# Attention scores that leave PSUM with their minimum: what does it do to the time?

## The chip, the cores and the metric

The kernel runs on one core of a Trainium2 chip. A time is the device time of one execution in microseconds. Before the change, three runs had a median of 697.19 us (697.01 to 699.52).

## The reference

q, k and v have shape (4, 8, 576, 64): batch, heads, sequence, head size. The reference rotates q and k by position, forms attention for each head, joins the heads to x of (4, 576, 512), and sends x through a token mixer and a channel mixer:

```
scores = (q_rot @ k_rot.T) / 8
scores = scores - max(scores, axis=-1)
attn   = exp(scores);  attn = attn / (sum(attn, axis=-1) + 1e-9)
x = attn @ v                                  # heads joined: (4, 576, 512)
u = x + (relu(x.T @ w_tok1) @ w_tok2).T       # 576 -> 256 -> 576
out = u + relu(u @ w_ch1) @ w_ch2             # 512 -> 1536 -> 512
```

The mixers' weights come as float64 and are split on the chip into pairs of fp32r values.

## The kernel before, in words

Attention goes over 16 pairs of heads. `prep` loads k, q and v of a pair, rotates k and q on POOL (pair 0 on DVE, L298 to L304), transposes them on PE (L327) and splits them into a high and a low part (ACT L341, DVE L344). `pair` takes the 576 rows of queries as four blocks of 128 and a tail of 64. The tail's rows of both heads are one block of 128, with block-diagonal operands made on POOL (L357). The order of blocks is 0, 1, tail, 2, 3.

For a block and each of its two heads: PE forms 128 x 576 scores in two PSUM banks (L429; the tail at L396) as three fp32r products. DVE takes the negated maximum of the row (L379), ACT the exponential with that as bias and the row's sum as an accumulator (L382), from PSUM into `p` in SBUF. PE transposes `p` in pieces of 64 (L449, tail L407), and ACT or DVE copies the pieces to `pt` (L454, L413, L420). After two or three blocks PE multiplies `pt` by v (L467, narrow with 256 columns after block 1, wide with 320 after block 3), and ACT or DVE copies the product out (L470). At the pair's end PE transposes it back (L496) and DVE scales it by 1/sum into `X` (L501, L505).

PSUM has 8 banks of 512 fp32 values for each partition. In attention two double banks (`s`) hold scores, and four single banks (`t`) hold transposes, two at a time, and P·V.

`plan` is a scheduler that runs when the program is built. Each task has an engine (or a choice of two), an estimated duration, the tasks it follows, the buffers it holds, and a priority. Repeatedly it takes, for each engine, the tasks that could start within SLACK of the earliest, and of these the one with the lowest priority. The resulting order of each engine's instructions is fixed: on the chip every engine works its queue from the front. AT holds what is added to 9 times the pair's number to make a priority. `f64_split` makes the mixers' weights; six blocks of token weights are split during attention, the channel weights during the mixers. The mixers follow in a plan of their own, with PSUM cut into 8 single banks.

Of the kernel before, what the change touches and what calls it, by code (L numbers as in the profile page):

```python
# [48 lines left out]
class Task:  # L49
    __slots__ = ("alts", "deps", "bufs", "prio", "end", "eng", "waits", "heirs", "mode")  # L50
# [5 lines left out]
class Plan:  # L56
# [8 lines left out]
    def add(self, eng, dur, fn, deps=(), bufs=(), prio=0.0, alts=(), mode="full"):  # L65
        t = Task()
        t.mode = mode
        t.alts = [(eng, dur, fn)] + list(alts)
        t.deps = [d for d in deps if d is not None]
        t.bufs = list(bufs)  # L70
        for b in t.bufs:
            b.users += 1
        t.prio = prio
        t.end = None
        t.heirs = []
        self.tasks.append(t)
        return t

    def start(self, t, eng):
# [11 lines left out]
        if eng == "PE" and t.mode != self.mode:  # L91
            s = max(s, self.clock["PE"] + SWITCH)
        return s

    def run(self):
# [10 lines left out]
        while left:  # L106
# [45 lines left out]
AT = {"qk": -239.14, "mx": 17.16, "ex": -436.59, "tr": -5.68, "eh": -55.41, "el": 296.2, "tt": -89.5, "th": -35.74, "tl": -123.52, "pv": -20.38, "p1": 280.88, "p2": -206.16, "fin": 18.15, "f6": -333.69, "load": -9.36, "rot": 238.0, "pt": -13.39, "bd": -69.91, "qkt": -64.88, "cp": 0.87, "dup": -248.71, "vs": 6.76}  # L152
FIRST = -60.0
SWITCH = 0.15
SLACK = {"PE": 0.08, "ACT": 0.06, "DVE": 0.32, "POOL": 0.17, "SP": 0.05}
# [18 lines left out]
def pool(n):  # L174
    return n * 0.00235 + 0.07
# [3 lines left out]
def rope_attention_mixer_kernel(ctx: ExitStack, tc: tile.TileContext, q, k, v, w_tok1, w_tok2, w_ch1, w_ch2, tab, out):  # L179
# [35 lines left out]
    def attention(ctx):  # L215
# [3 lines left out]
        def slots(nm, n, shape, dt=F32, pool=pers, fifo=True):  # L219
# [3 lines left out]
        raw = {"k": slots("kraw", 1, [P, 2, R + 1, D]), "q": slots("qraw", 1, [P, 2, R + 1, D]),  # L223
               "v": slots("vraw", 2, [P, 2, R + 1, D])}
# [3 lines left out]
        bds = slots("bd", 2, [P, 2, P], F32R)  # L228
# [35 lines left out]
        def prep(n):  # L264
            b, hp = divmod(n, HP)
            pos = 9 * n
            for nm, src, pr in (("k", k, 0.0), ("q", q, 0.5), ("v", v, 1.0)):
# [14 lines left out]
                pl = pos + AT["load"] + pr  # L282
# [27 lines left out]
                for r0, r1 in ((0, 2), (2, R + 1)) if n == 0 else ((0, R + 1),):  # L310
                    for i in range(4):
                        w = (r1 - r0) * 2 * D // (1 if i < 2 else 2)
                        bufs = [[rb, wb], [rb, ub], [ub, wb], [ub, wb]][i]
                        if n == 0:
                            x = [add("DVE", dve(w), rot(nc.vector, i, r0=r0, r1=r1), x, bufs, FIRST + pr + r0)]
                        else:
                            x = [add("POOL", pool(w), rot(nc.gpsimd, i), x, bufs, pos + AT["rot"] + pr)]
                    xy = [Buf(t_ps), Buf(t_ps)]
# [4 lines left out]
                    def tr(r0=r0, r1=r1, xy=xy, ub=ub, first=first):  # L323
                        for i in range(r1 - r0):
                            for z in range(2):
                                r = (i - 1) % (R + 1) if z and first else r0 + i
                                nc.tensor.transpose(xy[z].t[:, i * TL:(i + 1) * TL],  # L327
                                                    ub.t[halves[z], r].rearrange("p h d -> p (h d)"), ident[halves[z], halves[z]])

                    pp = pos + AT["pt"] + pr if n else FIRST + r0  # L330
                    t = add("PE", 0.11 * (r1 - r0), tr, x, [*xy, ub, hi, lo], pp, mode="row")
                    for z in range(2):
# [3 lines left out]
                        for o, m, i0 in parts:  # L336
                            src = lambda z=z, xy=xy, m=m, o=o: xy[z].t[:, o * TL:(o + m) * TL].rearrange("p (r s) -> p r s", s=TL)
# [8 lines left out]
                            y = add("ACT", act(m * TL), fh, [t], [xy[z], hi], pp)  # L346
                            eh.append(y)
                            el.append(add("DVE", dve(m * TL), fl, [y], [xy[z], hi, lo], pp))
                ready[n, nm] = (eh + el, hi, lo)
                if nm == "q":  # L350
                    bb = Buf(bds)
                    bdone = []
                    pp = pos + AT["bd"] + pr
# [10 lines left out]
        def pair(n):  # L364
# [13 lines left out]
            def mx(sb, nm):  # L378
                return lambda: nc.vector.tensor_reduce(out=nm.t, in_=sb.t[:, :, 0:W2], axis=AX.XY, op=ALU.max, negate=True)  # L379

            def ex(sb, nm, p, l):
                return lambda: nc.scalar.activation(out=p().rearrange("p (a b) -> p a b", a=2), in_=sb.t[:, :, 0:W2], func=ACTF.Exp,  # L382
                                                    bias=nm.t, accum_out=l())

            for i, j in enumerate(ORDER):
                g = 9 * n + 2 * i
                c = 0 if j in (0, 1) else 1
                if j is None:
                    xy = [Buf(t_ps), Buf(t_ps)]
                    sb, nm, pb = Buf(s_ps), Buf(nms), Buf(pqs)  # L390
# [6 lines left out]
                    x = add("PE", 0.81, qk, bdone + kd, [sb, bb, kh, kl], g + AT["qkt"])  # L397
                    x = add("DVE", 0.67, mx(sb, nm), [x], [sb, nm], g + AT["mx"])
                    x = [add("ACT", 0.65, ex(sb, nm, lambda pb=pb: pb.t[:, 0:S], lambda: lb.t[:, R, 0:1]),
                             [x], [sb, nm, pb, lb], g + AT["ex"])]  # L400
                    exps += x

                    def tr(pb=pb, xy=xy):
                        for r in range(R + 1):
                            for z in range(2):
                                c0 = r * P - (TL if z and r == R else 0)
                                nc.tensor.transpose(xy[z].t[:, r * TL:(r + 1) * TL], pb.t[halves[z], c0:c0 + P], ident[halves[z], halves[z]])  # L407

                    x = order_tr[0] = add("PE", 0.55, tr, [*x, order_tr[0]], [*xy, pb, pt[c]], g + AT["tr"], mode="row")
                    y = None  # L410
                    for z in range(2):
                        def cp(e, z=z, xy=xy, c=c, m=R + 1 - z):
                            return lambda: e(out=pt[c].t[:, (R + 1) * z:(R + 1) * z + m, 2 * P:2 * P + TL],  # L413
                                             in_=xy[z].t[:, 0:m * TL].rearrange("p (r s) -> p r s", r=m))

                        y0, y = y, both(cp, (R + 1 - z) * TL, [x], [xy[z], pt[c]], g + AT["cp"])
                        ev[c].append(y)

                    def cpt(e, xy=xy, c=c):
                        return lambda: e(out=pt[c].t[halves[1], R, 2 * P:2 * P + TL], in_=xy[1].t[halves[1], R * TL:(R + 1) * TL])  # L420
                    ev[c].append(both(cpt, TL, [x, y0], [xy[1], pt[c]], g + AT["cp"]))
                    continue
                sbs, nmb, pb = [Buf(s_ps), Buf(s_ps)], [Buf(nms), Buf(nms)], Buf(ps)
# [7 lines left out]
                t = add("PE", 0.8, qk, qd + kd, [*sbs, qh, ql, kh, kl], g + AT["qk"], mode="row")  # L431
                xs = []
                for h in range(2):
                    x = add("DVE", 0.67, mx(sbs[h], nmb[h]), [t], [sbs[h], nmb[h]], g + h + AT["mx"])
                    x = add("ACT", 0.65, ex(sbs[h], nmb[h], lambda h=h, pb=pb: pb.t[:, h * S:(h + 1) * S], lambda h=h, j=j: lb.t[:, j, h:h + 1]), [x],
                            [sbs[h], nmb[h], pb, lb], g + h + AT["ex"])
# [4 lines left out]
                for h in range(2):  # L441
                    xy = [Buf(t_ps), Buf(t_ps)]
                    m = R + h

                    def tr(pb=pb, xy=xy, h=h, m=m):
                        for i in range(m):
                            for z in range(2):
                                c0 = h * M + i * P
                                nc.tensor.transpose(xy[z].t[:, i * TL:(i + 1) * TL], pb.t[halves[z], c0:c0 + P], ident[halves[z], halves[z]])  # L449

                    x = order_tr[0] = add("PE", 0.11 * m, tr, [*xs[0:h + 1], order_tr[0]], [*xy, pb, pt[c]], g + h + AT["tr"], mode="row")
                    for z in range(2):
                        def cp(e, z=z, xy=xy, c=c, o=o, h=h, m=m):
                            return lambda: e(out=pt[c].t[:, R * h:R * h + m, o + z * TL:o + (z + 1) * TL],  # L454
                                             in_=xy[z].t[:, 0:m * TL].rearrange("p (r s) -> p r s", r=m))
                        ev[c].append(both(cp, m * TL, [x], [xy[z], pt[c]], g + h + AT["cp"]))
# [4 lines left out]
                ab = Buf(a_ps)  # L461

                def pv(c=c, w=w, ab=ab):
                    for r in range(R + 1):
                        for h in range(2):
                            m = pt[c].t[:, R if r == R else r + h * (R + 1), 0:w]
                            nc.tensor.matmul(ab.t[halves[h], 0:w], vb.t[:, h, r, :], m, start=(r == 0), stop=(r == R))  # L467

                def p1(e, w=w, ab=ab, c0=c0):
                    return lambda: e(out=oT.t[:, c0:c0 + w], in_=ab.t[:, 0:w])  # L470

                x = add("PE", 10 * (w / 1200 + 0.0025), pv, ev[c] + vdone, [ab, vb, pt[c]], g + AT["pv"], mode="col")
                pv_done.append(both(p1, w, [x], [ab, oT], g + AT["p1"]))

            pp = 9 * n + AT["fin"]
# [11 lines left out]
            x = add("ACT", 0.1, f1, exps, [lb], pp - 1)  # L487
            x = add("POOL", 0.1, f2, [x], [lb], pp - 0.9)
            inv = add("DVE", 0.13, f3, [x], [lb, rb], pp - 0.8)
            xy = [Buf(t_ps), Buf(t_ps)]  # L490
            cs = hp * 2 * D

            def f4():
                for j in range(R + 1):
                    for z in range(2):
                        nc.tensor.transpose(xy[z].t[:, j * D:(j + 1) * D], oT.t[halves[z], j * P:(j + 1) * P], ident[halves[z], halves[z]])  # L496

            x = add("PE", 0.55, f4, pv_done, [*xy, oT], pp, mode="row")
            for z in range(2):
                def f5(z=z):  # L500
                    nc.vector.tensor_tensor(out=X[b][:, :, cs + z * D:cs + (z + 1) * D], in0=xy[z].t[:, 0:R * D].rearrange("p (r d) -> p r d", r=R),  # L501
                                            in1=rb.t[:, 0:R, z].unsqueeze(2).to_broadcast([P, R, D]), op=ALU.mult)
# [357 lines left out]
```

## Time and profile before

| | us |
|---|---|
| median of 3 runs | 697.19 |
| the profiled execution | 696.52 |
| its span, first to last instruction | 694.7 |
| PE busy in it | 630.0 (91%) |
| DVE busy | 432.4 (62%) |
| ACT busy | 319.8 (46%) |
| POOL busy | 282.1 (41%) |

PE is TensorE's matmul, PEld its weight loads, DVE VectorE, ACT ScalarE, POOL GpSimd, SP the engine that issues most transfers. The busy shares are means over two unlike parts: attention ends near 325 us, and the mixers fill the rest.

### The profile page before, as it was taken

The page shows a single profiled execution, that of the slowest core. Times are in us where ns is not written, and L with a number is a line of the kernel's source. Part 1 is how long each engine was busy: PE and PEld are TensorE (multiplying, and loading weights), DVE is VectorE, ACT ScalarE, POOL GpSimd, SP SyncE. Part 2 cuts the span into 40 slices and gives each one's busy share as a digit, 9 for nine tenths or more (in the row PEclk, how much of TensorE's full clock was granted, in tenths as well). Part 3 has the DMA queues.
Part 4 walks back from the last instruction along what each step waited for, and adds up shares of the span by engine and source line. Part 5 has one row for each costly group of instructions (what it writes and reads, how often), then busy time and mean ns, then how long its engine had stood idle before and what let it go on. Part 6 is the DMA issues. An engine that isn't in the chain of part 4 may idle for free.

```text
span 694.7 us, 13160 instructions
## 1 busy us (share of the span) xinstructions
PE 630.0 (91%) x5112; PEld 529.2 (76%) x5112; DVE 432.4 (62%) x807; ACT 319.8 (46%) x808; POOL 282.1 (41%) x304
## 2 busy tenths in 40 slices
PE   2888878888888888888999999999999999999997
PEld 1676666666666666655887988989989989899895
DVE  4888986666666766665974888737842583322322
ACT  2777667666667776765452445412411321111010
POOL 2988865555556665002842546602700340000000
PEclk9999999999999999999999999999999999999999
DMA  6432212111222220200200223202210100001212
GB/s 184 130 88 63 56 41 56 49 45 58 56 57 56 57 57 19 87 2 1 85 30 1 60 74 94 77 0 83 70 31 0 61 1 0 1 1 45 76 61 91
DMA packets 33437, 36.56 MB, mean 53 GB/s; under 512 B 13792, under 2 KB 26848, under 8 KB 33376
## 3 DMA queue, kind: packets, MB, share of 16 engines
q1 hardware_dynamic: 32512, 35.01, 17.2%
q8 instruction: 40, 0.66, 0.4%
q10 hardware_dynamic: 864, 0.72, 0.3%
q14 instruction: 21, 0.17, 0.1%
HBM read 31.00 MB, written 4.72 MB: 51 GB/s over the span
## 4 chain that ended last, share of the span: by engine, by line
PE 74%; DVE 12%; ACT 9%; issue 2%; DMA 2%; SPq 0%; DVEq 0%; ACTq 0%
PE m L738 22%; PE m L761 22%; PE s L429 8%; PE t L467 8%; DVE nm L379 6%; ACT p L382 4%; PE m L677 4%; PE m L655 4%; PE t L449 4%; ACT pt L454 2%; DVE pt L454 2%; ACT pq L382 2%; PE s L396 1%; PE m L716 1%; DVE X L501 1%
## 5 line engine op out<-in xcount | busy, mean ns | idle before, releaser
L379 DVE TENSOR_REDUCE nm<-s 128x1 f32<-128x576 f32 x144 | 105.0, 749 | 71.2 <-PE s L429 68.3
L740 ACT ACTIVATE gh<-m 128x384 fp32r<-128x384 f32 x72 | 35.5, 492 | 190.7 <-PE m L738 167.6
L382 ACT ACTIVATE p<-s,nm 128x576 f32<-128x576 f32 x128 | 94.5, 741 | 14.4 <-DVE nm L379 12.3
L738 PE MATMUL m<-uh,c1h 128*128 128x384 f32 x288 | 97.0, 337 | 0.0
L738 PE MATMUL m<-uh,c1l 128*128 128x384 f32 x288 | 96.6, 336 | 0.0
L738 PE MATMUL m<-ul,c1h 128*128 128x384 f32 x288 | 96.6, 335 | 0.0
L467 PE MATMUL t<-pt,vraw 128*64 128x256 f32 (+1 forms) x640 | 92.6, 413 | 2.0 <-DVE pt L454 0.2
L761 PE MATMUL m<-c2h,gl 128*128 128x512 f32 x216 | 85.1, 394 | 0.0
L761 PE MATMUL m<-c2l,gh 128*128 128x512 f32 x216 | 85.0, 393 | 0.0
L761 PE MATMUL m<-c2h,gh 128*128 128x512 f32 x216 | 84.8, 393 | 0.0
L742 DVE SCALAR_TENSOR_TENSOR gl<-m,gh 128x384 fp32r<-128x384 f32 x72 | 39.6, 554 | 70.5 <-ACT gh L740 70.3
L763 DVE TENSOR_TENSOR X<-m,X 128x512 f32<-128x512 f32 x64 | 44.1, 690 | 58.6 <-PE m L761 58.6
L429 PE MATMUL s<-kh,qh 64*128 64x288 f32 x256 | 64.0, 352 | 17.9 <-ACT pq L382 14.1
L454 ACT COPY pt<-t 128x256 f32<-128x256 f32 (+1 forms) x160 | 57.9, 396 | 39.6 <-PE t L449 38.1
L467 PEld LDWEIGHTS t<-pt,vraw 128*64 128x64 f32 x640 | 57.0, 138 | 24.7 <-ACT pt L454 5.0
L449 PE MATMUL t<-ident,p 64*128 64x64 f32 x1152 | 60.0, 230 | 13.7 <-ACT p L382 6.4
L449 PEld LDWEIGHTS t<-ident,p 64*128 64x128 f32 x1152 | 52.9, 143 | 20.7 <-ACT p L382 14.7
L429 PEld LDWEIGHTS s<-kh,qh 64*128 64x128 f32 x256 | 37.8, 194 | 38.7 <-ACT pq L382 17.6
L738 PEld LDWEIGHTS m<-uh,c1h 128*128 128x128 f32 x288 | 54.1, 188 | 0.9
L738 PEld LDWEIGHTS m<-ul,c1h 128*128 128x128 f32 x288 | 54.1, 188 | 0.9
L738 PEld LDWEIGHTS m<-uh,c1l 128*128 128x128 f32 x288 | 54.1, 188 | 0.0
L429 PE MATMUL s<-kl,qh 64*128 64x288 f32 x256 | 52.4, 316 | 0.0
(120 smaller groups left out, 1235.5 us busy)
## 6 DMA issues: line engine op xcount, KB each, us to landing
stg<-in_moe_w_ch_dram SPq DMA_DIRECT2D x16, 384.0 KB, 3.2
stg<-in_moe_w_ch_dram SPq DMA_DIRECT2D x12, 512.0 KB, 4.1
kraw<-in_k_dram SPq DMA_DIRECT2D x16, 256.0 KB, 2.8
qraw<-in_q_dram SPq DMA_DIRECT2D x16, 256.0 KB, 2.8
vraw<-in_v_dram SPq DMA_DIRECT2D x16, 256.0 KB, 2.7
out_dram<-X SPq DMA_DIRECT2D x16, 256.0 KB, 2.3
stg<-in_moe_w_tok_dram SPq DMA_DIRECT2D x4, 512.0 KB, 3.9
kraw<-in_k_dram SPq DMA_DIRECT2D x32, 32.0 KB, 2.6
```

The costliest lines, as they stand in the source:

```text
L379: return lambda: nc.vector.tensor_reduce(out=nm.t, in_=sb.t[:, :, 0:W2], axis=AX.XY, op=ALU.max, negate=True)
L382: return lambda: nc.scalar.activation(out=p().rearrange("p (a b) -> p a b", a=2), in_=sb.t[:, :, 0:W2], func=ACTF.Exp, bias=nm.t, accum_ou ...
L429: nc.tensor.matmul(sbs[h].t[:, c, 0:W2], flat(a.t)[halves[h], TL + j * P:TL + (j + 1) * P], flat(m.t)[halves[h], TL * (1 - h) + c * W2:TL ...
L449: nc.tensor.transpose(xy[z].t[:, i * TL:(i + 1) * TL], pb.t[halves[z], c0:c0 + P], ident[halves[z], halves[z]])
L454: return lambda: e(out=pt[c].t[:, R * h:R * h + m, o + z * TL:o + (z + 1) * TL], in_=xy[z].t[:, 0:m * TL].rearrange("p (r s) -> p r s", r=m))
L467: nc.tensor.matmul(ab.t[halves[h], 0:w], vb.t[:, h, r, :], m, start=(r == 0), stop=(r == R))
L655: nc.tensor.matmul(tb.t, a, m, start=(r == 0 and i == 0), stop=(r == R and i == len(lst) - 1))
L738: nc.tensor.matmul(tb.t[:, 0:N], a, m, start=(i == 0), stop=(i == len(lst) - 1))
L740: x = add("ACT", 0.49, lambda f=f, tb=tb: nc.scalar.activation(out=gb.t[0][:, f], in_=tb.t[:, 0:N], func=ACTF.Relu), [x], [tb, gb], pr + f)
L742: y = add("DVE", 0.56, lambda f=f, tb=tb: nc.vector.scalar_tensor_tensor(out=gb.t[1][:, f], in0=tb.t[:, 0:N], scalar=0.0, in1=gb.t[0][:, f ...
L761: nc.tensor.matmul(tb.t, a, m, start=(i == 0), stop=(i == len(lst) - 1))
L763: y = add("DVE", 0.69, lambda u=u, tb=tb: nc.vector.tensor_tensor(out=u, in0=tb.t, in1=u, op=ALU.add), [z] + sums.get((ci, x), []), [tb], ...
```

## The change

The row's minimum of the negated scores replaces the negated maximum of the scores. One DVE instruction multiplies the scores by -1, writes them to `p` in SBUF and gives their minimum as its accumulator output. The exponential then reads `p` and writes `p`, with scale -1.

PSUM in attention becomes four double banks (`d`), which scores, transposes, P·V and the output's transposes share; a pair of transposes that took two single banks takes one double bank, and P·V takes a double bank and uses half of it. Second copies of raw q and k, and further copies of v, `bd`, `p`, `pq`, `oT`, `l`, `ri` and `nm` are added.

AT gets a priority for each block and half in place of one for each kind of task, and one for each of the six token blocks. SLACK and estimated durations are changed. The planner gets a flag `port`: such a DVE task starts after POOL's last planned task, and POOL's next one after it. Pair 0's rotation and the DVE steps of `f64_split` carry it. The planner works only when the program is built.

```
-AT = {"qk": -239.14, "mx": 17.16, "ex": -436.59, "tr": -5.68, ...}
+AT = {'load': [-278.24, -272.1, 339.05], ..., 'qk': [-463.94, -272.15, -138.15, -195.59, -137.37],
+  'mx': [-688.94, -39.61, -686.19, ...], ..., 'tok': [239.05, 84.91, 118.65, 92.86, -136.8, -17.46], ...}
-SLACK = {"PE": 0.08, "ACT": 0.06, "DVE": 0.32, "POOL": 0.17, "SP": 0.05}
+SLACK = {'PE': 0.304, 'ACT': 0.099, 'DVE': 0.027, 'POOL': 0.008, 'SP': 0.284}
 def start(self, t, eng):
+        if eng == "DVE" and t.port:
+            s = max(s, self.clock["POOL"])
 def run(self):
+            if eng == "DVE" and t.port:
+                self.clock["POOL"] = max(self.clock["POOL"], end)
-        raw = {"k": slots("kraw", 1, ...), "q": slots("qraw", 1, ...), "v": slots("vraw", 2, ...)}
+        raw = {"k": slots("kraw", 2, ...), "q": slots("qraw", 2, ...), "v": slots("vraw", 3, ...)}
-        ps = slots("p", 3, [P, 2 * S])
-        pqs = slots("pq", 1, [P, S + TL])
+        ps = slots("p", 4, [P, 2 * S])
+        pqs = slots("pq", 2, [P, S + TL])
-        nms = slots("nm", 4, [P, 1])
-        s_ps = slots("s", 2, [P, 2, 512], pool=psum)
-        t_ps = slots("t", 4, [P, 512], pool=psum, fifo=False)
-        a_ps = t_ps
+        nms = slots("nm", 8, [P, 1])
+        d_ps = slots("d", 4, [P, 2, 512], pool=psum, fifo=False)
-            def mx(sb, nm):
-                return lambda: nc.vector.tensor_reduce(out=nm.t, in_=sb.t[:, :, 0:W2], axis=AX.XY, op=ALU.max, negate=True)
-            def ex(sb, nm, p, l):
-                return lambda: nc.scalar.activation(out=p().rearrange("p (a b) -> p a b", a=2), in_=sb.t[:, :, 0:W2], func=ACTF.Exp,
-                                                    bias=nm.t, accum_out=l())
+            def mx(sb, nm, p):
+                return lambda: nc.vector.tensor_scalar(out=p().rearrange("p (a b) -> p a b", a=2), in0=sb.t[:, :, 0:W2], scalar1=-1.0,
+                                                       scalar2=None, op0=ALU.mult, op1=ALU.min, accum_out=nm.t)
+            def ex(nm, p, l):
+                return lambda: nc.scalar.activation(out=p(), in_=p(), func=ACTF.Exp, bias=nm.t, scale=-1.0, accum_out=l())
-                    x = add("DVE", 0.67, mx(sbs[h], nmb[h]), [t], [sbs[h], nmb[h]], g + h + AT["mx"])
-                    x = add("ACT", 0.65, ex(sbs[h], nmb[h], ...), [x], [sbs[h], nmb[h], pb, lb], g + h + AT["ex"])
+                    x = add("DVE", 0.74, mx(sbs[h], nmb[h], p), [t], [sbs[h], nmb[h], pb], at("mx", h))
+                    x = add("ACT", 0.74, ex(nmb[h], p, ...), [x], [nmb[h], pb, lb], at("ex", h))
-                    xy = [Buf(t_ps), Buf(t_ps)]
+                    xy = Buf(d_ps)
-                    x = order_tr[0] = add("PE", 0.11 * m, tr, ...)
+                    x = order_tr[0] = add("PE", 0.062 * m + 0.02, tr, ...)
-                ab = Buf(a_ps)
+                ab = Buf(d_ps)
 def f64_split(...)
-        x = add("DVE", 0.0021 * n + 0.05, mul_(nc.vector), [x, z], [cb, ab], prio, alts=[("POOL", pool(n), ...)])
+        x = add("DVE", 0.0012 * n + 0.07, mul_(nc.vector), [x, z], [cb, ab], prio, port=True, alts=[("POOL", pool(n), ...)])
...
-            tok_weights(pos)
+            tok_weights(iter(AT["tok"]))
```

## Rows read from the trace of the kernel before

**Rows 1.** By stretch: start:end, length; busy us of PE, PEld, DVE, ACT, POOL; clock; DMA.

```profile
0.00:39.16 39.16, 20.96 (x219) 17.48 (x220) 26.71 (x57) 19.96 (x55) 23.58 (x43) 0.97 0.51 144
39.16:61.31 22.15, 18.53 (x217) 15.12 (x217) 19.82 (x35) 16.94 (x47) 19.00 (x21) 0.89 0.28 82
61.31:80.80 19.49, 16.20 (x207) 12.48 (x207) 18.31 (x34) 14.03 (x39) 17.43 (x19) 1.00 0.23 61
80.80:101.48 20.68, 16.33 (x206) 12.23 (x207) 16.84 (x34) 13.93 (x39) 14.64 (x17) 1.00 0.13 39
101.48:304.20 202.72, 176.99 (x2249) 136.90 (x2249) 134.31 (x287) 141.60 (x395) 104.72 (x133) 1.00 0.19 53
175.09:193.50 18.41, 16.12 (x206) 12.54 (x206) 12.25 (x27) 12.89 (x36) 10.72 (x14) 1.00 0.20 52
304.20:326.60 22.40, 17.99 (x202) 12.24 (x203) 11.34 (x27) 13.12 (x36) 1.26 (x2) 1.00 0.01 1
326.60:384.96 58.36, 57.90 (x257) 46.08 (x258) 42.23 (x67) 23.42 (x46) 30.69 (x21) 0.97 0.11 35
384.96:694.70 309.74, 305.15 (x1561) 276.64 (x1559) 162.82 (x273) 76.82 (x156) 70.81 (x54) 1.00 0.15 46
```

**Rows 2.** Chain of waits in one pair, 175.09 to 193.50: start, us, what.

```profile
175.09 3.33 PE t L467 x20
...
180.30 0.84 ACT p L382 x2
...
182.34 0.77 DVE nm L379
...
183.14 0.84 ACT pq L382 x2
...
184.02 0.95 PE s L429 x10
...
187.23 0.84 ACT p L382 x2
```

**Rows 3.** Timeline of PE's weight loads: start, us, what, idle before and releaser.

```profile
178.35 0.18 PEld L429 LDWEIGHTS s<-kh,qh 64*128 64x128 f32 x2 [0.49 <-issue]
...
179.12 0.71 PEld L449 LDWEIGHTS t<-ident,p 64*128 64x128 f32 x18
...
181.18 0.30 PEld L396 LDWEIGHTS s<-kh,bd 128*128 128x128 f32 x2 [0.40 <-ACT p L382]
...
184.02 0.18 PEld L429 LDWEIGHTS s<-kh,qh 64*128 64x128 f32 x1 [1.11 <-ACT pq L382]
...
185.31 1.93 PEld L467 LDWEIGHTS t<-pt,vraw 128*64 128x64 f32 x20
...
188.11 0.18 PEld L429 LDWEIGHTS s<-kh,qh 64*128 64x128 f32 x1 [0.30 <-ACT p L382]
```

**Rows 4.** Groups of instructions, whole execution: busy us, mean ns, then idle before.

```profile
L379 DVE TENSOR_REDUCE nm<-s 128x1 f32<-128x576 f32 x144 | 105.0, 749 | 71.2 <-PE s L429 68.3 <-PE s L396 2.0
...
L382 ACT ACTIVATE p<-s,nm 128x576 f32<-128x576 f32 x128 | 94.5, 741 | 14.4 <-DVE nm L379 12.3
...
L454 ACT COPY pt<-t 128x256 f32<-128x256 f32 (+1 forms) x160 | 57.9, 396 | 39.6 <-PE t L449 38.1
...
L382 ACT ACTIVATION_READ_ACCUMULATOR p<-s,nm 128x1 f32 x128 | 25.3, 198 | 0.0
...
L555 ACT CAST c2h<-fh 128x512 fp32r<-128x512 f32 x12 | 7.5, 625 | 1.6 <-POOL fh L549 0.8 <-DVE fh L549 0.8
...
L660 ACT ACTIVATE rs<-m 128x512 fp32r<-128x512 f32 x8 | 4.3, 593 | 11.9 <-PE m L655 11.9
...
L485 DVE RECIPROCAL ri<-l 128x10 f32<-128x10 f32 x16 | 3.3, 208 | 1.2 <-POOL l L482 1.2
```

**Rows 5.** Timeline near 52 us: a DVE instruction beside one of POOL.

```profile
52.31 1.54 POOL L300 TENSOR_TENSOR uq<-qraw,tabs 128x640 f32<-128x640 f32 x1
52.40 1.74 DVE L543 SCALAR_TENSOR_TENSOR fh<-stg,fa 128x256 uint32<-128x256 uint32 x1
```

More of the change, by code (lines that the diff above doesn't have):

```diff
@@ L49 @@
 class Task:
-    __slots__ = ("alts", "deps", "bufs", "prio", "end", "eng", "waits", "heirs", "mode")
+    __slots__ = ("alts", "deps", "bufs", "prio", "end", "eng", "waits", "heirs", "mode", "port")
 LAG = {"PE": 0.2, "ACT": 0.14, "DVE": 0.12, "POOL": 0.12, "SP": 1.8}
@@ L63, in __init__, with add @@
         self.mode = None
-    def add(self, eng, dur, fn, deps=(), bufs=(), prio=0.0, alts=(), mode="full"):
+    def add(self, eng, dur, fn, deps=(), bufs=(), prio=0.0, alts=(), mode="full", port=False):
         t = Task()
         t.mode = mode
+        t.port = port
         t.alts = [(eng, dur, fn)] + list(alts)
@@ L174, in pool @@
 def pool(n):
[L175 removed]
+    return n * 0.00235 + 0.08
 @with_exitstack
@@ L466, in pv @@
                             m = pt[c].t[:, R if r == R else r + h * (R + 1), 0:w]
-                            nc.tensor.matmul(ab.t[halves[h], 0:w], vb.t[:, h, r, :], m, start=(r == 0), stop=(r == R))
+                            nc.tensor.matmul(ab.t[halves[h], 0, 0:w], vb.t[:, h, r, :], m, start=(r == 0), stop=(r == R))
                 def p1(e, w=w, ab=ab, c0=c0):
[L470 to L475, printed above, removed]
+                    return lambda: e(out=oT.t[:, c0:c0 + w], in_=ab.t[:, 0, 0:w])
+                x = add("PE", 10 * (w / 1200 + 0.0025), pv, ev[c] + vdone, [ab, vb, pt[c]], g + AT["pv"][c], mode="col")
+                pv_done.append(both(p1, w, [x], [ab, oT], g + AT["p1"][c]))
+            pp, pi, pf = (9 * n + AT[k][0] for k in ("fin", "inv", "f6"))
             rb = Buf(ris)
@@ L485, in f3 @@
                 nc.vector.reciprocal(out=rb.t, in_=lb.t)
[L487 to L490, printed above, removed]
+            x = add("ACT", 0.1, f1, exps, [lb], pi)
+            x = add("POOL", 0.1, f2, [x], [lb], pi)
+            inv = add("DVE", 0.13, f3, [x], [lb, rb], pi)
+            xy = Buf(d_ps)
             cs = hp * 2 * D
@@ L545, in f64_split @@
-        x = add("DVE", 0.0014 * n + 0.05, lambda: TS(out=AU(), in0=HU(), scalar1=0xFF800000, scalar2=None, op0=ALU.bitwise_and),
-                [x], [ab, hb], prio)
+        x = add("DVE", 0.0007 * n + 0.06, clamp(nc.vector), [x], [ab], prio, port=True, alts=[("POOL", pool1(n), clamp(nc.gpsimd))])
+        x = add("DVE", 0.0007 * n + 0.06, lambda: TS(out=AU(), in0=AU(), scalar1=3, scalar2=None, op0=ALU.logical_shift_left),
+                [x], [ab], prio, port=True)
+        x = add("DVE", 0.0012 * n + 0.07, lambda: STT(out=HU(), in0=hi_w(), scalar=0x80000000, in1=AU(), op0=ALU.bitwise_and,
+                                                     op1=ALU.bitwise_or), [x], [sb, ab, hb], prio, port=True)
@@ L547, in f64_split @@
+        x = add("DVE", 0.0007 * n + 0.06, lambda: TS(out=AU(), in0=HU(), scalar1=0xFF800000, scalar2=None, op0=ALU.bitwise_and),
+                [x], [ab, hb], prio, port=True)
         mul_ = lambda e: lambda: e.tensor_tensor(out=A(), in0=C(), in1=A(), op=ALU.mult)
[L548 removed]
+        x = add("DVE", 0.0012 * n + 0.07, mul_(nc.vector), [x, z], [cb, ab], prio, port=True, alts=[("POOL", pool(n), mul_(nc.gpsimd))])
@@ L554, in f64_split @@
             at = lambda o: o() if callable(o) else o
-            y = add("ACT", act(n, True), lambda hi=hi, src=src: nc.scalar.copy(out=at(hi), in_=src()), [x], [hb, *kept], prio)
+            y = add("ACT", n / 1060 + 0.18, lambda hi=hi, src=src: nc.scalar.copy(out=at(hi), in_=src()), [x], [hb, *kept], prio)
             sub = lambda e, hi=hi, lo=lo, src=src: lambda: e.tensor_tensor(out=at(lo), in0=src(), in1=at(hi), op=ALU.subtract)
-            done += [y, add("DVE", 0.0021 * n + 0.05, sub(nc.vector), [y], [hb, *kept], prio, alts=[("POOL", pool(n), sub(nc.gpsimd))])]
+            done += [y, add("DVE", 0.0012 * n + 0.07, sub(nc.vector), [y], [hb, *kept], prio, port=True, alts=[("POOL", pool(n), sub(nc.gpsimd))])]
         return done
```

117 lines of the change are left out of this document (54 added, 63 removed).

## The prediction

> **What bounds the kernel now.** I read the busy time by stretches first, because the core does two unlike jobs [rows 1]. From 326.6 us to the end (the mixers) PE is busy 305.15 of 309.74 us in the last stretch and 57.90 of 58.36 us in the one before: it is the bound there, and the change touches only the planner's costs for work beside it. Before 326.6 us lies attention. From 101.48 to 304.20 us eleven pairs repeat, 202.72 / 11 = 18.43 us each; in one of them PE is busy 16.12 us, DVE 12.25, ACT 12.89, POOL 10.72 [rows 1]. No engine is full, so an order of waits sets the period. From 39.16 to 101.48 us three pairs take 20.8 us each: the token weights are split there, and DVE is busy 54.97 of 62.32 us.
>
> The chain of waits inside one pair (175.09 to 193.50 us) names that order [rows 2]. Three times it goes from ACT's exponential (L382, 0.84 us with the read of its accumulator) straight to matmuls of scores: at 180.30, 183.14 and 187.23. The reader is to see that PE needs nothing that the exponential computes; it waits for the PSUM bank that the exponential still reads. The weight loads of PE say the same: they stood idle 0.40, 1.11 and 0.30 us for ACT before those scores [rows 3]. Two double banks hold all scores, one per half pair, and each is free only after scores, minimum and exponential in a row.
>
> **The change part by part.**
>
> *The bank's release.* The minimum now leaves the scores in SBUF, so the bank is free one exponential earlier. Off the chain: three times 0.84 us plus about 0.04 us of issue, 2.64 us a pair [rows 2]. What is late next is DVE: the same chain holds four minima of about 0.77 us (182.34 is one) with copies and products queued ahead of them, and those stay. Bounds: nothing, if the same exponential is waited for somewhere else, to all PE idleness (below).
>
> *The minimum itself.* 144 reductions of 128x576 at 749 ns [rows 4] become 144 scalar instructions over the same elements, with an accumulator. The main part I take at the same 749 ns, one element after the other out of PSUM. No accumulator of DVE is in this trace. On ACT the 741 ns exponential is followed by a read of 198 ns, and the two take 0.84 us of the chain, so the read costs 0.10 us there [rows 2, 4]. From below: nothing, or a little less than nothing if the scalar form starts sooner than the reduction; from above: DVE's smallest row, 208 ns for 128x10 [rows 4]. I take 0.10 us, the nearest kind of instruction: 0.9 us more DVE work a pair (12.25 to 13.2), and 0.40 us more on the chain, for its four minima. The Trainium skill, "VectorE: DVE Perf Modes" (Two Vector instructions with no wait between them), says that an operation that also writes its accumulator out is two instructions, the main one and a read. The trace shows that on ACT only; by a fused single instruction the chain would be 0.4 us shorter.
>
> *Writing 576 elements into SBUF beside POOL.* POOL is at the rotations 10.72 of 18.41 us [rows 1], and one DVE instruction shows what a collision costs: a 128x256 one beginning at 52.40 lasts 1.74 us, ending just after POOL's at 52.31 does [rows 5]. It reads two SBUF tensors; the minimum reads one PSUM tensor. The reductions, which write nearly nothing, don't show it. Bounds: 0 to about 1 us for each minimum; I take 0, as the copies out of PSUM are written to SBUF too and keep their 0.4 us beside POOL. The Trainium skill, "SBUF — State Buffer" (Who interferes with whom), counts the scalar form with an accumulator output out of those that lock POOL's port. No row here shows that form; by the opposite rule the minima would pay what the third rival charges.
>
> *The exponential in place.* It reads SBUF instead of PSUM. Two ACT rows of 128x512 to fp32r differ so: 625 ns from SBUF (L555), 593 from PSUM (L660) [rows 4]. 0.03 us each, bounds 0 to 0.05: 0.3 us a pair on ACT, which has 5.5 us idle in a pair and is off the new chain. No minus sign costs anything: the scale rides in the instruction.
>
> *Four shared double banks.* Before, two double banks held scores and four single ones transposes and P·V. Now all nineteen users of a pair draw from four double banks, and P·V takes two banks for one. Time held, worked from the rows: eight score halves, 0.77 us of matmuls (178.35 to 179.12) and one or two minima, about 2.2 us on average, 17.6; the tail's 1.8; nine transposes with their copies (0.71 [rows 3] and two of 0.40 [rows 4]), about 1.5 each, 13.5; P·V 2.8 and 3.8 with their copies; output and two rotations, 5.5. Together 45 bank-us, of 64.8 that four banks have in 16.2 us: 69%. So it fits, but not always when wanted. Cost 0 in the forecast, up to one transposes' hold a half pair in the third rival.
>
> *More buffers, loads, token weights, order.* Second and third copies of raw inputs, probabilities and sums only let work start earlier. SP issues the same loads; the DMA engines are 0.19 busy in the steady stretch [rows 1], which hides any collision (bound 0 to 1 us in all). The token weights' six blocks get priorities of their own; they cost DVE 54.97 - 3 x 12.25 = 18 us in the three early pairs. With 13.2 us a pair and DVE at best 18.31/19.49 = 94% full [rows 1], a 16.2 us pair leaves it 2.0 us for them, so they spread over more pairs. I take 1 us off each of the three, bounds 0 and 4.6 (down to 16.2).
>
> *The mixers.* Cheaper planner prices for DVE will draw splits of the channel weights from POOL (70.81 us there) to DVE, which is 162.82 of 309.74 us busy [rows 1]. PE's full row hides it: 0, bounds -1 to +3.
>
> **The sum.** Per pair 18.41 - 2.64 + 0.40 = 16.2 us; eleven pairs give 11 x 2.2 = 24 us, the early three 3, and the first pair (to 39.16) and last (from 304.20) 1 each, as they have the same waits among others: 29. The profiled execution took 696.52 us, span 694.7 and 1.8 around it; minus 29 is 667.3. The median of the runs is 0.7 above it: 668.
>
> PE's own floor limits what more may come. Its dense pieces [rows 3]: scores 4 x 0.77, the tail's about 0.8, transposes 4 x 0.71 and four tens of 0.5, P·V about 2.3 and 2.8 (its narrow loads 1.93, the wide 5/4 of that, with the change of mode behind each): 13.9 to 14.5 us a pair.
>
> **Rivals.**
> 1. *PE becomes the bound.* With four banks, scores run ahead of DVE and the pair falls to about 14.8 us: 3.6 x 11 and 3 to 6 for the rest, 650. For it: DVE's 13.2 and ACT's 13.2 would fit. Against: 13.2 of 14.8 leaves DVE 89% full, as in the early pairs, which were slow. Chance 0.18.
> 2. *Half is lost to the next wait.* Transposes wait for the same exponential, copies and products stay ahead of the minima on DVE, or minima with 0.21 us reads: 1.0 to 1.2 us a pair off, 13 us in all with the early pairs unchanged, 684. For it: PE's loads show only 1.8 us of idleness for these three waits, not 2.6 [rows 3]. Chance 0.18; another 0.05 for nothing gained, 697: the change then frees the bank without anyone using it sooner.
> 3. *Slower: scores wait for the shared banks.* Scores of a half pair need two free banks at once. If transposes or P·V are handed one just ahead, the scores wait for 0.71 us of transposes and two copies, some 1.5 us. It decides from 2.2 us a pair (one and a half such waits). Two of them give -2.24 + 3.0 = +0.8 us a pair, 15 pairs, 12 us: 709. For it: 69% held and a fixed order of waits on estimated durations. Against: before, scores waited for their own banks three times a pair too. A minimum locked out by POOL (0.6 us and more each) would end there as well. Chance 0.10.
>
> **How the numbers follow.** The forecast has 0.49, with a range of its own of 658 to 680 (a pair of 15.5 to 17.2 us). Adding rivals 1 and 2 the range is 647 to 692; left out are the no-gain case, the slower one and a little below. A measurement of this kernel tells 0.5% (3.5 us) from no change. Faster: 0.49 + 0.18 + 0.18 = 0.85; same 0.05; slower 0.10.
>
> **What would show it.** Right: the period between the wide P·V is near 16.2 us; no wait of score matmuls for ACT remains; minima of about 750 ns with a short read behind each; the mixers' last stretch as long as before; token work on DVE past 101 us. Wrong: minima above 0.9 us beside POOL (port), score matmuls idle for copies out of PSUM (rival 3), PE idle under 1 us a pair (rival 1), or a longer first 39 us because token splits go ahead of the first rotation on DVE.

## The result and the profile after

The changed kernel takes 651.57 us (median of 4 runs, 649.93 to 653.17); the kernel before took 697.12 beside it. The ratio is 0.9339, 95% interval 0.9307 to 0.9371: 45.6 us faster, where I had forecast 29. The time lies in the range, 16 us under the forecast and at rival 1's figure (650), and outside the forecast's own range (658 to 680). The profiled execution took 649.93 us, span 647.8, clock 0.994.

By stretches, the kernel after, columns as in [rows 1]. The cuts are the starts of the wide P·V (the twenty instructions with 320 columns) and the mixers' first matmul, as before:

```profile
0.00:42.70 42.70, 25.79 (x325) 21.00 (x325) 28.39 (x82) 26.63 (x73) 26.03 (x50) 0.96 0.53 146
42.70:82.20 39.50, 36.77 (x494) 28.01 (x495) 35.05 (x94) 35.76 (x101) 33.53 (x39) 1.00 0.29 85
82.20:252.57 170.37, 161.98 (x2268) 121.63 (x2267) 145.77 (x403) 146.80 (x410) 123.94 (x150) 1.00 0.22 62
206.29:221.72 15.43, 14.72 (x208) 11.03 (x207) 12.17 (x36) 12.77 (x37) 10.73 (x14) 1.00 0.10 30
252.57:273.45 20.88, 17.83 (x213) 10.86 (x213) 9.86 (x30) 9.05 (x27) 0.25 (x1) 1.00 0.01 2
273.45:337.50 64.05, 59.29 (x257) 45.95 (x258) 48.95 (x80) 20.98 (x42) 18.32 (x13) 0.97 0.11 31
337.50:647.80 310.30, 305.58 (x1561) 276.63 (x1559) 164.95 (x314) 76.51 (x156) 15.92 (x13) 1.00 0.15 46
```

Against [rows 1], with the forecast in brackets. The first cut doesn't part the same work: before it PE does 325 instructions where it did 219, and from there to 82.20 us the wide P·V comes round twice, not three times, as PE now runs further ahead. So the first two rows are read together: 82.20 us against 101.48, -19.3 us, with 819 and 849 PE instructions done. The kernel before had 819 done at 99.95 us, so for the same work this is -17.8 us (-4: the first pair 1, the early three 3). The eleven pairs 170.37 - 202.72 = -32.4, 15.49 us each (-24, 16.2 each); the rest of attention 20.88 - 22.40 = -1.5 (-1); the mixers' first stretch 64.05 - 58.36 = +5.7 (0); the last stretch +0.6 (0). The spans differ by 46.9 us. In one steady pair PE is busy 14.72 of 15.43 us; before it was 16.12 of 18.41, with as many instructions. Part of that is inside the wide P·V: its twenty instructions took 3.33 us [rows 2], and those at 206.29 us take 2.91.

The waits of PE's weight loads in the eleven pairs show that the three waits of [rows 3] went. Each row: engine, buffer and line, what it waited for, total us, times, longest. First the kernel before, 101.48 to 304.20 us:

```profile
PEld s L429 <- ACT pq L382: 12.2, 11, 1.1
PEld t L449 <- ACT p L382: 7.3, 11, 1.2
PEld s L396 <- ACT p L382: 4.5, 11, 0.4
PEld s L429 <- ACT p L382: 3.6, 12, 0.3
```

Then the kernel after, 82.20 to 252.57 us, the longest ones but for one more row of issue:

```profile
PEld d L453 <- issue: 5.8, 12, 0.5
PEld d L433 <- ACT pt L458: 3.5, 10, 0.4
...
PEld d L453 <- ACT pt L424: 2.6, 8, 0.4
```

Scores (L433) no longer wait for the exponential. They wait for the copy of a transposed block (`pt`) out of the shared bank: rival 3's mechanism, but 0.35 us each and once a pair, not 1.5 us twice.

The changed instructions, groups of the kernel after (busy us, mean ns, idle before them):

```profile
L386 ACT ACTIVATE p<-p,nm 128x576 f32<-128x576 f32 x128 | 99.1, 781 | 0.6 <-DVE p L382 0.2
L382 DVE TENSOR_SCALAR_CACHE_REDUCE p<-d 128x576 f32<-128x576 f32 x128 | 90.6, 754 | 12.8 <-PE d L433 12.7
...
L382 DVE DVE_READ_ACCUMULATOR p<-d 128x1 f32 x128 | 10.6, 83 | 0.0
```

And a timeline of the same kernel (start, duration), two minima in a row beside a POOL instruction:

```profile
160.42 0.75 DVE L382 TENSOR_SCALAR_CACHE_REDUCE p<-d 128x576 f32<-128x576 f32 x1
160.53 0.87 POOL L307 TENSOR_TENSOR uq<-uq,w 128x320 f32<-128x320 f32 x1
...
161.10 0.08 DVE L382 DVE_READ_ACCUMULATOR p<-d 128x1 f32 x1
161.10 0.75 DVE L382 TENSOR_SCALAR_CACHE_REDUCE p<-d 128x576 f32<-128x576 f32 x1
```

The reader is to see three things. A minimum takes 754 ns where the reduction took 749. Its read takes 83 ns, but the next minimum starts with it, 0.68 us after the last one's start. And neither minimum takes longer beside POOL, which is at work on SBUF in the same time.

### The profile page after: what moved, and what is told of

Read it like the earlier page. It is cut to its first block, busy times and chain, and to the rows that moved or that the text cites. A ratio compares the mean times of both kernels' runs of the same rounds, so it can differ in the third digit from the quotient of the medians.

```text
span 647.8 us, 13219 instructions
## 1 busy us (share of the span) xinstructions
PE 607.2 (94%) x5112; PEld 504.1 (78%) x5112; DVE 433.0 (67%) x999; ACT 315.7 (49%) x805; POOL 218.0 (34%) x265
## 4 chain that ended last, share of the span: by engine, by line
PE 51%; DVE 3%; ACT 0%; issue 0%
PE m L742 23%; PE m L765 22%; PE m L681 3%; PE m L659 2%; PE m L720 1%; DVE xs L642 1%; DVE rs L667 0%; DVE xs L640 0%; DVE ul L723 0%; DVE fh L553 0%; DVE c2l L560 0%; DVE fh L547 0%; DVE c1l L560 0%; DVE gl L746 0%; DVE fa L545 0%
## 5 line engine op out<-in xcount | busy, mean ns | idle before, releaser
L386 ACT ACTIVATE p<-p,nm 128x576 f32<-128x576 f32 x128 | 99.1, 781 | 0.6 <-DVE p L382 0.2
L382 DVE TENSOR_SCALAR_CACHE_REDUCE p<-d 128x576 f32<-128x576 f32 x128 | 90.6, 754 | 12.8 <-PE d L433 12.7
L471 PE MATMUL d<-pt,vraw 128*64 128x256 f32 (+1 forms) x640 | 84.4, 411 | 0.5 <-ACT pt L424 0.4
L471 PEld LDWEIGHTS d<-pt,vraw 128*64 128x64 f32 x640 | 43.2, 137 | 29.7 <-DVE p L382 2.2
L433 PE MATMUL d<-kh,qh 64*128 64x288 f32 x256 | 59.2, 337 | 4.2 <-ACT pt L458 2.2
L453 PEld LDWEIGHTS d<-ident,p 64*128 64x128 f32 x1152 | 46.2, 139 | 16.7 <-issue 7.2
L453 PE MATMUL d<-ident,p 64*128 64x64 f32 x1152 | 53.9, 227 | 4.7 <-ACT pt L458 1.8
L458 ACT COPY pt<-d 128x320 f32<-128x320 f32 (+1 forms) x158 | 55.0, 404 | 6.4 <-PE d L453 3.6
L433 PE MATMUL d<-kl,qh 64*128 64x288 f32 x256 | 52.2, 311 | 0.3 <-DVE kl L347 0.3
L553 POOL TENSOR_TENSOR fh<-fh,fa 128x384 f32<-128x384 f32 (+3 forms) x11 | 11.3, 1027 | 118.2 <-DVE fa L551 118.2
```

Of the source, the lines that this page charges most:

```text
L382: return lambda: nc.vector.tensor_scalar(out=p().rearrange("p (a b) -> p a b", a=2), in0=sb.t[:, :, 0:W2], scalar1=-1.0, scalar2=None, op0 ...
L386: return lambda: nc.scalar.activation(out=p(), in_=p(), func=ACTF.Exp, bias=nm.t, scale=-1.0, accum_out=l())
L433: nc.tensor.matmul(sbs[h].t[:, c, 0:W2], flat(a.t)[halves[h], TL + j * P:TL + (j + 1) * P], flat(m.t)[halves[h], TL * (1 - h) + c * W2:TL ...
L453: nc.tensor.transpose(xy.t[:, z, i * TL:(i + 1) * TL], pb.t[halves[z], c0:c0 + P], ident[halves[z], halves[z]])
L471: nc.tensor.matmul(ab.t[halves[h], 0, 0:w], vb.t[:, h, r, :], m, start=(r == 0), stop=(r == R))
```

## The experiments

Where an edit alters a task of the planner, the whole order is planned anew, with priorities that were set for the kernel that it starts from. Such a run (all but the two with a shorter P·V and the one with the memset) measures the edit and the order that comes of it. Times of before in these batches were 698.1 to 699.8 us.

**1. The release alone**, in the kernel before: old PSUM split, old priorities and buffers.

```
-    ...tensor_reduce(out=nm.t, in_=sb.t[:, :, 0:W2], ..., op=ALU.max, negate=True)
+    ...tensor_scalar(out=p()..., in0=sb.t[:, :, 0:W2], scalar1=-1.0, ..., op0=ALU.mult, op1=ALU.min, accum_out=nm.t)
-    ...activation(out=p()..., in_=sb.t[:, :, 0:W2], func=ACTF.Exp, bias=nm.t, ...)
+    ...activation(out=p(), in_=p(), func=ACTF.Exp, bias=nm.t, scale=-1.0, ...)
```

> The kernel before with one edit: the minimum writes the negated scores to SBUF and the exponential works there in place. PSUM (two double banks for scores, four single ones for the rest), priorities and prices stay. Theory A (the bank's early release is the gain, the rest serves it): a pair falls from 18.4 us to 16.2 to 16.8 us, 665 to 675 us in all. Theory B (the new order and prices are the gain): 688 us or more, since the old order was chosen for the old waits. Theory C (sharing the banks is the gain): 685 to 697 us.

684.89 us, ratio 0.981 (0.9759 to 0.986). Its waits of weight loads, 101 to 300 us, and two starts of the wide P·V, nine periods apart:

```profile
PEld t L468 <- DVE XT L506: 12.1, 11, 1.2
...
PEld t L450 <- DVE kl L344: 6.5, 10, 0.7
PEld t L450 <- ACT p L383: 5.7, 22, 0.4
PEld s L396 <- DVE p L379: 4.8, 11, 0.4
```

```profile
98.74 3.28 PE L468 MATMUL t<-pt,vraw 128*64 128x320 f32 x20
...
259.92 3.29 PE L468 MATMUL t<-pt,vraw 128*64 128x320 f32 x20
```

(259.92 - 98.74) / 9 = 17.91 us a pair: 0.5 us less than before, of the 2.2 forecast. The scores' waits for the exponential went as forecast, and others came in their place, 29.1 us in these four rows where the four of before make 27.6: P·V (L468) for DVE's output copy `XT`, transposes (L450) for DVE's copy `kl` and for the exponential, scores for the minimum. This is rival 2's mechanism. That its time (684) came out as well is in part luck: it asked for 1.0 to 1.2 us a pair. Eleven pairs from 98.74 us give 3.3 us (199.43 against 202.72, one of the later ones being longer); the rest of the gain lies before them and at the end of attention.

**2. Everything but the release**: the old minimum and exponential in the kernel after, with its banks, buffers and priorities.

> The changed kernel with the old minimum and exponential: the scores' bank is held until the exponential has read it. Shared banks, new order, prices and buffers stay. Theory A: PE waits for exponentials again, 680 to 697 us. Theory B: under 665 us. Theory C: under 665 us.

703.63 us, 1.0057 (1.0027 to 1.0088). The waits between 101 and 304 us again show the exponential, now before the transposes:

```profile
PEld d L453 <- ACT p L385: 19.5, 30, 1.2
...
PEld d L433 <- ACT p L385: 5.4, 11, 0.5
```

So the release is necessary: without it the rest gains nothing in all. The loss isn't all waits. Two pairs in a row, columns as in [rows 1], the first at clock 1.00:

```profile
227.01:244.97 17.96, 15.37 (x208) 11.07 (x207) 12.60 (x27) 12.47 (x35) 9.74 (x13) 1.00 0.19 54
244.97:264.40 19.43, 16.86 (x209) 11.93 (x207) 12.51 (x27) 12.57 (x35) 11.86 (x15) 0.91 0.13 34
```

At clock 1.00 the pair is 0.5 us shorter than before (18.41) and 2.5 longer than with the release; what the lower clock of other pairs adds isn't shown apart.

**3. No sharing**: two double banks for the scores, two for the rest.

```
-        d_ps = slots("d", 4, [P, 2, 512], pool=psum, fifo=False)
+        s_ps = slots("s", 2, [P, 2, 512], pool=psum)
+        d_ps = slots("t", 2, [P, 2, 512], pool=psum, fifo=False)
...
-                sbs, nmb, pb = [Buf(d_ps), Buf(d_ps)], [Buf(nms), Buf(nms)], Buf(ps)
+                sbs, nmb, pb = [Buf(s_ps), Buf(s_ps)], [Buf(nms), Buf(nms)], Buf(ps)
```

> The changed kernel with its four double banks divided: two for scores, two for transposes and products. Release, new order, prices and buffers stay. Theory A: scores still need their own two banks only until the minima are done, 655 to 665 us. Theory B: 652 to 658 us. Theory C: 675 us or more, with score matmuls waiting for DVE's minima.

721.01 us, 1.0324 (1.0276 to 1.0372). One pair, columns as in [rows 1]:

```profile
174.91:195.30 20.39, 16.46 (x206) 11.62 (x206) 12.25 (x35) 13.56 (x38) 10.69 (x13) 0.92 0.19 49
```

The clock is lower here too (0.92 in this pair); how much of the loss that makes isn't shown.

**4. Neither release nor sharing**, only the new priorities, prices and buffers: both edits of 2 and 3.

> The changed kernel without the release and without the sharing: old minimum and exponential, two double banks for scores, two for the rest; new order, prices and extra buffers alone. Theory A: 685 to 700 us. Theory B: 655 to 670 us. Theory C: 685 to 700 us.

814.1 us, 1.1654 (1.1601 to 1.1706), clock 0.887. By itself the new order loses. Sharing under the old priorities wasn't tried, nor were the new attention priorities taken out of the full change, so what the order alone brings to the whole isn't shown.

**5 and 6. Is PE the bound?** Twelve of the twenty narrow P·V instructions of each pair left out (the output lacks that part), in the kernel before and in the kernel after; the order stays.

```
-                    for r in range(R + 1):
+                    for r in ((0, R) if c == 0 else range(R + 1)):
```

> The kernel before without three fifths of the narrow product P·V (6 of its 10 matmul calls; the output lacks their part). The order of all the rest stays. The calls take about 0.107 us per weight load in the row, 12 loads, 1.28 us of PE a pair, 20 us in 16 pairs. Theory P (waits bound the kernel before, PE bounds the changed one): the narrow product is off the chain of waits, 0 to 5 us less, 692 us or more. Theory Q (PE was nearly the bound before as well): 678 to 684 us.

> The changed kernel with the same 1.28 us of PE a pair left out of the narrow product (6 of 10 matmul calls; the output lacks their part), the order of all the rest as it is. Theory P (PE is now the bound): 16 to 20 us less, 632 to 636 us. Theory D (DVE and ACT, 79 and 83% busy in a pair, hold PE back through their queues): 0 to 6 us less, 646 to 652 us.

The kernel after: 645.58 us, 0.9232 (0.9205 to 0.9258), 6 us faster. Two of its pairs:

```profile
191.75:206.62 14.87, 13.65 (x195) 10.36 (x194) 12.13 (x36) 12.74 (x37) 11.54 (x15) 1.00 0.25 69
206.62:221.56 14.94, 13.68 (x196) 10.38 (x195) 12.17 (x36) 12.76 (x37) 10.78 (x14) 1.00 0.14 42
```

PE's busy time in a pair falls from 14.72 to 13.65 and 13.68, 1.1 us; the period from 15.43 to 14.87 and 14.94, 0.5 us. PE's work sets about half a microsecond of the pair, and another limit lies right under it. Over all eleven pairs (82.77 to 251.64 us) the run gains 1.5 us, as one of them, at clock 0.90, takes 17.58 us.

The kernel before: 715.44 us, 1.0231 (1.02 to 1.0262). It is slower with less work, which neither theory had. Two of its pairs:

```profile
104.08:124.29 20.21, 17.18 (x195) 13.87 (x194) 12.21 (x27) 12.89 (x37) 11.05 (x14) 0.84 0.18 51
219.76:238.17 18.41, 14.89 (x195) 11.66 (x195) 12.16 (x27) 12.89 (x36) 10.74 (x14) 1.00 0.20 54
```

Where the clock is at 1.00, the pair takes 18.41 us, as before, with 1.2 us less PE work: the narrow P·V isn't on the chain of waits, and PE didn't bound this kernel. Where the clock is lower, the pair is longer; the last section returns to that.

**7. Is DVE the bound?** A memset of 128x64, needed by nothing, behind each of the 144 minima of the kernel after.

```
+                    nc.vector.memset(scr, 0.0)
```

> The changed kernel with a needless DVE instruction (a memset of 128x64 to a tile that nobody reads) behind each of the 144 minima, the order as it is. About 0.12 us of DVE queue each, estimated from the 0.13 us that DVE's smallest rows take from start to start: 1.1 us a pair, 17 us in all. Theory P: DVE has 3 us idle in a pair, 652 to 657 us. Theory D: 662 to 670 us.

650.2 us, 0.9294 (0.9267 to 0.9322): no change. The memsets add up to 16.1 us (112 ns each), but that isn't 16.1 us more of DVE's time. Two minima with a memset between them:

```profile
205.98 0.69 DVE L384 TENSOR_SCALAR_CACHE_REDUCE p<-d 128x576 f32<-128x576 f32 x1
...
206.64 0.11 DVE L386 MEMSET scr<- 128x64 f32 x1
206.67 0.69 DVE L384 TENSOR_SCALAR_CACHE_REDUCE p<-d 128x576 f32<-128x576 f32 x1
```

The second minimum starts 0.03 us after the memset and 0.69 us after the first one, where it was 0.68 without a memset. Over the execution DVE is busy 435.8 us in place of 433.0. So this shows only that 2.8 us more of DVE's time, about 0.2 us a pair, cost nothing; the test is too light to tell whether DVE bounds the pair.

**8. The mixers' prices**: in the kernel after, `f64_split` of the channel weights is planned with the old durations and without `port`; the token weights keep the new ones.

```
+        ch = bool(kept)
+        pt_ = not ch
+        c1, c2, c3 = (..., 0.0021 * n + 0.05) if ch else (..., 0.0012 * n + 0.07)
...
-        x = add("DVE", 0.0012 * n + 0.07, mul_(nc.vector), [x, z], [cb, ab], prio, port=True, ...)
+        x = add("DVE", c3, mul_(nc.vector), [x, z], [cb, ab], prio, port=pt_, ...)
```

> The changed kernel with the planner's old prices (and no port rule) for the splits of the channel weights alone; attention and token splits keep the new ones. Theory M (the stretch from the first mixer matmul to the first channel matmul, 64.05 us against 58.36, is longer because those splits moved from POOL to DVE ahead of the token mixer's own DVE steps): 645 to 648 us. Theory N (it is longer because attention ends with less prepared, xs and token splits among it): 651 to 653 us.

644.6 us, 0.9217 (0.919 to 0.9244). The mixers:

```profile
273.76:333.98 60.22, 59.20 (x257) 46.90 (x258) 42.94 (x66) 25.23 (x50) 26.38 (x19) 0.95 0.11 33
333.98:644.10 310.12, 305.35 (x1560) 276.64 (x1559) 163.41 (x271) 77.04 (x156) 72.46 (x56) 1.00 0.15 46
```

3.8 of the 5.7 us come back, as POOL takes such steps again (26.38 and 72.46 us busy in place of 18.32 and 15.92). The spans differ by 3.7 us, the medians by 7.0; the ratio's interval lies below that of the change. This version beats both kernels.

**9. The token weights' prices**: the reverse of 8, old durations and no `port` for the token weights alone.

> The changed kernel with the planner's old prices and no port rule for the splits of the token weights alone (channel weights keep the new ones). Theory T (the 23 us won in the three early pairs come from splits that no longer crowd DVE beside POOL): the early pairs lengthen again, 660 us or more. Theory U (they come from the freed and shared banks, which let PE run ahead whatever DVE does in between): 650 to 655 us.

671.48 us, 0.9616 (0.9578 to 0.9654), 20 us slower than the change.

```profile
80.00:120.00 40.00, 32.04 (x380) 22.84 (x382) 28.46 (x76) 27.46 (x78) 26.73 (x31) 0.83 0.13 37
120.00:160.00 40.00, 37.79 (x534) 27.86 (x532) 30.91 (x89) 32.71 (x94) 25.61 (x34) 1.00 0.22 62
198.08:213.51 15.43, 14.71 (x208) 11.04 (x207) 12.16 (x36) 12.77 (x37) 10.70 (x14) 1.00 0.22 65
```

The late pairs keep 15.43 us; the loss is all in the early part. There the splits crowd into 17.7 to 97 us again, and PE does 380 instructions at clock 0.83 where forty later microseconds hold 534.

**10. The token weights' places**: the old priorities for the six blocks, new prices.

```
-            tok_weights(iter(AT["tok"]))
+            tok_weights(iter([38.0, 56.0, 74.0, 92.0, 110.0, 128.0]))
```

> The changed kernel with the token blocks' old priorities (38, 56, 74, 92, 110, 128 in place of 239.05 to -17.46); prices and the port rule stay new. Theory T: the splits crowd early again, 658 us or more. Theory U: 650 to 655 us.

659.94 us, 0.9433 (0.9378 to 0.9487): 8 us, again mostly early: the fourth wide P·V starts at 106.17 us where it started at 97.42.

**11 and 12. The buffers.** First all the old counts in the kernel after (raw k and q 1, v 2, `bd` 2, `p` 3, `pq` 1, `oT` 2, `l` 3, `ri` 2, `nm` 4), then only `p` 3, `pq` 1 and `nm` 4, which the minimum fills.

> The changed kernel with the buffer counts of before in SBUF (raw k and q 1, v 2, bd 2, p 3, pq 1, oT 2, l 3, ri 2, nm 4); PSUM, instructions and priorities as changed. Theory B1 (scores run ahead only because probabilities have a fourth and a second buffer to be written to, since the minimum now fills them): 665 us or more. Theory B2 (the extra copies are idle): 650 to 656 us.

> The changed kernel with the old counts of the buffers that the minimum now fills (p 3 in place of 4, pq 1 in place of 2, nm 4 in place of 8); raw inputs, bd, oT, l and ri keep the new counts. With all counts old it took 680.5 us and 17.1 us a pair. Theory B1 (the release needs somewhere to put the scores: these buffers carry the 29 us): 670 us or more, a pair near 17 us. Theory B3 (the loads, rotations and results of neighbouring pairs carry them): 658 us or less, a pair near 15.5 us.

680.49 us, 0.9747 (0.9703 to 0.9791), and 668.31, 0.959 (0.9551 to 0.9628). One pair of 11, then one of 12:

```profile
184.00:201.05 17.05, 15.68 (x207) 11.33 (x208) 11.62 (x33) 13.59 (x39) 10.77 (x13) 1.00 0.21 58
```

```profile
202.45:219.29 16.84, 15.78 (x206) 11.38 (x207) 11.56 (x34) 13.61 (x39) 10.75 (x14) 1.00 0.23 58
```

The extra buffers are worth 29 us and 1.6 us a pair; the three that the minimum fills have 17 of the 29 and 1.4 of the 1.6. That lies between the two theories on them: most of the pair's gain goes with those three, but not all of the total.

## Why the forecast was right in direction and short by a third

*What bounds the kernel.* Right: the bank held through the exponential cost the wait, PE wasn't the bound (experiment 5), and the release is what the rest needs (experiment 2). That the time lies in the range is in part luck all the same: rival 1 had put 650 there with a pair of 14.8 us that PE bounds, which isn't what came.

*"Off the chain: 2.64 us a pair."* This step failed as an addition to the old order. The term was too large from the start, as the chain goes straight from the exponential to scores twice and not three times. Behind the one at 180.30 stands DVE's output product:

```profile
181.18 0.75 DVE X L501 x2
```

The tail's weight loads wait there too, 0.40 us [rows 3], but the chain goes on through DVE. By that reading the term is 2 x 0.88 = 1.76 us. In the old order 0.5 us a pair came out (experiment 1), because the same matmuls, or those behind them, met waits that had been hidden: `XT`, `kl`, the minimum. I had named DVE as what is late next, and then counted its minima only, not its copies ahead of P·V. The lower bound (nothing) and rival 2 held the truth for the release alone.

*"More buffers only let work start earlier", cost 0.* The mis-sized term that matters most: 29 us with the order planned anew (experiment 11). The minimum now needs a free `p` before it can free the bank, so with three `p` and one `pq` the released bank should wait for a buffer that transposes still read. The traces don't show that wait as such: in the pair of experiment 12 the minima's longest waits are 0.5 us for scores and 0.4 us for an exponential, so the loss sits in the order planned around the missing buffers, and its mechanism stays argued. I had costed the wait that the change adds at nothing without asking what holds that buffer.

*The eleven pairs.* 15.49 us, between the forecast's 16.2 and rival 1's 14.8. PE is idle 0.71 us of 15.43, which I had named as rival 1's sign; but experiment 6 gives back only 0.5 us for 1.1 us of PE work, so PE alone isn't the bound. Experiment 7 put too little on DVE to tell about it. What holds the pair at 14.9 us then (DVE's 12.17 or ACT's 12.77 busy us in the fixed order, or the shared banks) stays open. Rival 1's objection, a DVE 89% full, doesn't arise: it is 79% full.

*"I take 1 us off each of the three."* For the first pair and these three together 17.8 us came instead of 4; even with my bound for the three (3 x 4.6 = 13.8) it would be 14.8. That bound stopped at the forecast's pair and saw no gain in the clock: the first of these pairs had 0.89 and 18.53 us of PE work, the next two 1.00 and 16.20 and 16.33 [rows 1], so the clock cost it some 2 us, an estimate from these rows; after 42.70 us it is 1.00. Token work on DVE now reaches to 177 us (a step of L549 at 177.47), as forecast in kind.

The new prices and `port` for it are worth 20 us (experiment 9; the two weren't parted) and its places 8 (experiment 10), each with the rest of the change in place. This, not a PE-bound pair, took the time to rival 1's figure.

*The minimum.* The 749 ns held (754). The read exists and costs nothing in a row of minima, where I had 0.10 us. The Trainium skill, "VectorE: DVE Perf Modes" (Two Vector instructions with no wait between them), says that such an operation is two instructions; the trace agrees, with 754 and 83 ns. DVE's 13.2 busy us a pair came out as 12.17.

*POOL's port.* 0 held: 0.75 us beside POOL. That agrees with the Trainium skill, "SBUF — State Buffer" (Who interferes with whom), which counts this form out of those that lock the port.

*The exponential in place.* 781 - 741 = 40 ns; I took 30, bounds 0 to 50. ACT stays at 12.77 busy us of the pair (12.89 before).

*Shared banks at 0.* Right for the order given: one wait of 0.35 us a pair. (The working lists 23 users of the banks, not nineteen; its 45 bank-us are the sum of that list.) But the sharing is no neutral edit: taken away it costs 69 us (experiment 3), in an order made for it.

*The mixers at 0, bounds -1 to +3.* +6.3, above the bound. The reasoning "PE's full row hides it" fails at the start of the mixers, where PE waits for DVE's steps of the token mixer (`rs`: L667 makes the low part of its hidden layer). Timeline of PE, kernel after, idle before and its releaser in brackets:

```profile
302.15 0.73 PE L681 MATMUL m<-rs,w2h 128*128 128x512 f32 x2 [1.78 <-DVE rs L667]
...
303.92 0.50 PE L681 MATMUL m<-rs,w2h 128*128 128x512 f32 x1 [0.58 <-DVE rs L667]
```

The chain of waits shows what DVE does meanwhile. Ahead of the 1.78 us wait stand its own steps for `xs`, the two parts of the mixer's input; ahead of the 0.58 us wait, between two steps for `rs`, a step of a channel-weight split (`c1l`):

```profile
301.16 0.34 DVE xs L640
301.50 0.60 DVE rs L667
302.10 1.18 DVE c1l L560
```

POOL, which can take such steps of both kinds, is busy 18.32 us in this stretch where it was 30.69. With the channel splits at the old prices (experiment 8, whose lines stand five further down) these waits go, and with them most of the 5.7 us. First the kernel after, 273.4 to 340 us, then that run, 273.7 to 335:

```profile
PE m L681 <- DVE rs L667: 3.3, 4, 1.8
```

```profile
PE m L686 <- DVE rs L672: 0.2, 1, 0.2
```

Taken one at a time from the change, the parts cost 52 (release), 69 (sharing), 29 (buffers), 20 and 8 us (token weights): 178 where the whole gives 46. They are no sum; each needs the others, and each removal also spoils an order made for all.

## What to carry to other kernels

Freeing a buffer earlier is worth what the next thing in line can do with it: count the buffer that the earlier release now needs, the copies queued ahead on the engine that frees it, and the order of work, before multiplying the wait by its number. A planner's price that helps one phase is to be looked at in each phase that uses it; here the token weights gained 20 us by it, and the channel weights lost 4 to 7 (spans, medians). A stretch with a low granted clock may give back more than its waits. And a group's added busy time isn't time added to its engine: look at the starts in a row before calling an engine free.

## What the runs showed of the hardware that I had not expected

Less TensorE work made the kernel before slower (experiment 5). Its stretches show where; columns as in [rows 1]:

```profile
92.00:96.00 4.00, 1.62 (x15) 0.74 (x11) 3.88 (x6) 1.26 (x3) 2.68 (x4) 0.98 0.00 0
96.00:100.00 4.00, 3.04 (x34) 2.93 (x34) 1.72 (x4) 2.16 (x7) 0.00 (x0) 0.50 0.01 4
100.00:104.00 4.00, 4.00 (x49) 3.74 (x49) 2.67 (x6) 3.03 (x10) 3.05 (x4) 0.50 0.14 42
104.00:108.00 4.00, 4.00 (x24) 2.90 (x22) 1.84 (x5) 2.21 (x6) 3.68 (x7) 0.74 0.15 42
108.00:112.00 4.00, 3.58 (x52) 3.00 (x53) 2.75 (x8) 2.90 (x8) 3.84 (x4) 1.00 0.54 150
```

PE is busy 1.62 us of the four from 92 us on, at 2.4 GHz (0.98); then the clock stands at 1.2 GHz (0.50) for eight microseconds in which PE is busy 7.04 us, and is back at 1.00 from 108. From 120 us the same comes again. Over the run the granted clock is 0.943, against 0.991 before. With 1.2 and 2.4 GHz as its two levels, these means make about 80 us at the lower one, against some 12 before, an estimate from the two spans. Of this run's pairs from 104.08 to 298.27 us the three at 1.00 take 18.4 us as before, and the seven that take longer have a lower clock (20.21 at 0.84, experiment 5). That fits a loss through the clock, but no run held the clock fixed, so how much of the 16 us it makes isn't shown. The 6 us of experiment 6 stand at a lower clock too (0.986 against 0.994); its two pairs above, at 1.00, are the cleaner price.
